# Five engines in hand-written order, load casts on GpSimd, unit 2 loaded ahead of the last weight piece, units 6 and 7 transposed by DMA: chunked attention followed by a bilinear FFN

## The chip, the cores and the metric

One core of one Trainium2 chip. The metric is the device time of one execution in microseconds (us). Traces and profiles are of one execution each. Their span is some 2 us shorter than the device time (338.6 against about 340.4 us for the kernel before).

## The reference

```python
# q, k, v: [8, 8, 576, 64] float32; w_a, w_b: [512, 1536]; w_out: [1536, 512]
q_c, k_c, v_c = (t.reshape(8, 8, 9, 64, 64) for t in (q, k, v))       # chunks of 64 tokens
scores = q_c @ k_c^T / 8
attn = softmax(scores)                                                # within a chunk
x = (attn @ v_c) put to [4608 tokens, 512]
return ((x @ w_a) * (x @ w_b)) @ w_out                                # float32
```

So there are 4608 tokens. The attention is small, and the three matrix products are nearly all of the arithmetic.

## The kernel before: the parts that matter here

Tokens go through in 18 *units* of 256 for the attention and in 9 *blocks* of 512 (two units each) for the FFN. For a unit, q, k and v are loaded in float32 and cast to bf16. Then q and k are transposed, either by TensorE through PSUM (units below `PE_UNITS`) or by the DMA queue. `scores`, `sums` and `values` are TensorE matmuls. Between them ScalarE takes exponents, the logarithm of the sums and the exponent of its negative, and VectorE multiplies. The result is the unit's half of `xT`. An `ab_step` makes one of twelve pieces of the hidden layer of a block: four matmuls each with w_b and w_a, an eviction on ScalarE and a product on VectorE. An `out_step` is twelve matmuls with w_out.

```python
    def cast_ab(i):                                   # a piece of the weights, 256 columns
        for n in ("wb", "wa"):
            w_ab[n, i] = wpool.tile([128, NKT, WCOL], BF16, name=f"{n}{i}")
            nc.vector.tensor_copy(out=w_ab[n, i], in_=staged.pop((n, i)))
    # ... (cast_wo likewise)
    def cast(U, names="qkv"):
        for n in names:
            raw[n, U] = raw_pool.tile([128, 2, H, D], BF16, name=f"{n}_raw", ...)
            eng = nc.vector if U < PE_UNITS else nc.gpsimd          # PE_UNITS = 8
            eng.tensor_copy(out=raw[n, U], in_=staged.pop((n, U)))

    def transpose_pe(U):
        # ... 8 transpositions of q, 8 of k into PSUM, then copies out:
            for i in range(2):
                cp = nc.vector.tensor_copy if w == 0 else nc.scalar.copy
                cp(out=dst[:, i], in_=tp[:, i].rearrange("c m (g p) -> c m g p", g=2))

    def slot(s=None, f=None):                         # scores of unit s, the rest of unit f
        # ... sums(f); scores(s); values(f)

    # Only TensorE and the sync queue follow the program; the other engines' order
    # is chosen by a scheduler when the program is built.
    with tc.manual_schedule(engines={mybir.EngineType.PE, mybir.EngineType.SP}):
        load_qk(0); load_qk(1); load_v(0); load_v(1)            # (one per line in the file)
        for i in range(3):
            load_ab(i)
        cast(0, "qk")
        transpose_pe(0)
        slot(0)
        cast(1, "qk")
        transpose_pe(1)
        cast(0, "v")
        slot(1, 0)
        cast(1, "v")
        cast_ab(0)
        slot(None, 1)
        for i in range(NWP):                                    # NWP = 6: block 0
            # ... cast_ab(i + 1), load_ab(i + 3), load(2) and load(3) at i == 3
            ab_step(0, 2 * i)
            if i == 5:
                # ... loads of w_out
                load(4)
                cast(2, "qk")
                load_qk(5)
                transpose_pe(2)
            ab_step(0, 2 * i + 1)
        slot(2)                                                 # unit 2, alone
        cast(2, "v")
        load_v(5)
        slot(None, 2)
        # ... block 1 in halves of 256 columns, with units 3 to 6 in between; blocks 2 to 8
```

The softmax here doesn't subtract the row's maximum and nothing guards it: scores larger than these inputs give would overflow.

## Time and profile before

| | before |
|---|---|
| device time, median (range) | 340.86 us (340.47 to 341.51, 3 runs) |
| span of the profiled execution | 338.6 us |
| TensorE busy | 313.0 us, 92% |
| VectorE, ScalarE, GpSimd busy | 158.9, 129.8, 31.9 us |
| first projection matmul | 22.31 us |
| one block of 512 tokens, blocks 3 to 7 | 33.2 us |

In the profile, PE is TensorE, DVE is VectorE, ACT is ScalarE, POOL is GpSimd and SPq is the sync queue, which issues the DMAs. L280 are the projection matmuls (`ab_step`), L296 the output matmuls, L164 the transpositions, L194, L209 and L232 the scores, sums and values.

The page of the kernel before starts with busy times per engine. Below them, one digit stands for the busy tenths of each of 40 equal slices of the span. PEclk is the granted TensorE clock in tenths.

```profile
PE 313.0 (92%) x2709; PEld 160.6 (47%) x2744; DVE 158.9 (47%) x251; ACT 129.8 (38%) x227; POOL 31.9 (9%) x36
...
PE   2459959999999999999999999999999999999994
...
PEclk9999996999999999999999999999999999999999
```

TensorE is nearly full from slice 7 on. The holes are in the first three slices (to 25 us) and in slice 6 (42 to 51 us), and in slice 7 the clock drops. The steady part has no hole. These lines are from the chain that ended last of the kernel before (start us, length us, what), from the sums of one unit to those of the next unit but one. The sums return every 33.17 us.

```profile
119.26 0.34 PE ps L209 x4
...
152.43 0.34 PE ps L209 x4
```

The start of the kernel before is in its timeline (start us, length us, engine, line, operation, output<-input, count; in brackets the idle time just before and what ended it).

```profile
7.74 0.69 DVE L152 CAST q_raw<-q_in 128x1024 bf16<-128x1024 f32 x1 [0.82 <-DMA q_in<-in_q_dram]
8.05 1.32 ACT L172 COPY qkt<-ps 128x512 bf16<-128x512 bf16 x2 [6.03 <-PE ps L164]
9.28 0.69 DVE L152 CAST k_raw<-k_in 128x1024 bf16<-128x1024 f32 x1 [0.84 <-DMA k_in<-in_k_dram]
...
9.88 1.32 DVE L172 COPY qkt<-ps 128x512 bf16<-128x512 bf16 x2
...
11.26 0.64 PE L194 MATMUL ps<-qkt 64*64 64x64 bf16 x32 [3.25 <-DVE qkt L172]
...
22.31 0.59 PE L280 MATMUL ps<-xT,wb_307 128*128 128x512 bf16 x1 [3.10 <-DVE xT L241]
```

The two casts at 7.74 and 9.28 are of unit 1. VectorE does them, and waits for the loads of them, while unit 0's transposed q lies ready in PSUM. Its copy runs only at 9.88, and TensorE's first scores wait for it.

Between blocks 0 and 1, the timeline of TensorE before shows unit 2 alone.

```profile
45.56 0.45 PE L194 MATMUL ps<-qkt 64*64 64x64 bf16 x32
...
46.70 0.90 PE L209 MATMUL ps<-E,ones 64*64 64x512 bf16 x4 [0.69 <-ACT E L202]
...
47.20 0.65 PE L232 MATMUL ps<-E,v_raw 64*64 64x64 bf16 x32
...
51.14 1.01 PE L280 MATMUL ps<-xT,wb_307 128*128 128x256 bf16 x4 [3.30 <-DVE xT L241]
```

The windows view of the kernel before (columns: stretch, its length, busy us and count per engine from PE to POOL, granted clock, DMA share, GB/s) gives the clock of that hole and of the stretch behind it.

```profile
47.80:51.10 3.30, 0.04 (x5) 0.07 (x1) 1.30 (x3) 1.94 (x3) 0.00 (x0) 0.74 1.06 406
51.10:56.40 5.30, 5.26 (x28) 3.79 (x28) 2.04 (x4) 1.12 (x3) 0.00 (x0) 0.52 1.21 257
```

So there are three things to see: two waits of TensorE (0.69 and 3.30 us), and after them 5.3 us in which it is busy but at half its clock.

### The profile page before, as it was taken

How to read it: one execution, taken by the hardware profiler on the slowest of the kernel's cores; microseconds unless marked ns; L12 is line 12 of the kernel's file. 1: busy time of each engine (PE TensorE's matmuls, PEld its weight loads, DVE VectorE, ACT ScalarE, POOL GpSimd, SP SyncE). 2: the span in 40 equal slices, each digit the busy share in tenths (PEclk: the TensorE clock that was granted, in tenths of full speed). 3: DMA queues.
4: the chain of work that ended last, by engine and by line, in shares of the span. 5: the costliest groups of instructions: out<-in, count | busy, mean ns of one | idle time of the engine just before them, and what ended most of it. 6: DMA issues, size and time to landing. Idle time of an engine off the chain costs nothing.

```text
span 338.6 us, 6687 instructions
## 1 busy us (share of the span) xinstructions
PE 313.0 (92%) x2709; PEld 160.6 (47%) x2744; DVE 158.9 (47%) x251; ACT 129.8 (38%) x227; POOL 31.9 (9%) x36
## 2 busy tenths in 40 slices
PE   2459959999999999999999999999999999999994
PEld 1324437876644444444444444444444444444441
DVE  2558665876854343435343434343435343533331
ACT  2643363645635162516341633253334424312200
POOL 0000000000333213312212130000000000000000
PEclk9999996999999999999999999999999999999999
DMA  8999999949999999998839863241111112011213
GB/s 238 328 345 286 255 375 230 290 107 260 222 238 220 192 217 244 232 219 187 199 70 202 204 157 75 52 95 33 31 37 27 33 31 48 16 31 45 50 32 93
DMA packets 130783, 52.87 MB, mean 156 GB/s; under 512 B 102080, under 2 KB 124608, under 8 KB 130752
## 3 DMA queue, kind: packets, MB, share of 16 engines
q1 hardware_dynamic: 130752, 52.44, 63.5%
q8 instruction: 21, 0.34, 0.4%
q14 instruction: 10, 0.08, 0.1%
HBM read 37.75 MB, written 9.44 MB: 139 GB/s over the span
## 4 chain that ended last, share of the span: by engine, by line
PE 90%; ACT 3%; DMA 2%; DVE 1%; issue 1%; SPq 1%
PE ps L280 56%; PE ps L296 27%; PE ps L164 2%; DMA k_in<-in_k_dram 2%; PE ps L209 2%; PE ps L194 2%; PE ps L232 1%; ACT rs L222 1%; ACT ln L219 1%; ACT qkt L172 1%; SPq L128 1%; DVE xT L241 1%; ACT E L202 0%; DVE qkt L172 0%; DVE k_raw L152 0%
## 5 line engine op out<-in xcount | busy, mean ns | idle before, releaser
L288 ACT CAST b_sb<-ps 128x512 bf16<-128x512 f32 (+1 forms) x120 | 64.3, 546 | 145.3 <-PE ps L280 121.6
L289 DVE TENSOR_TENSOR ab_sb<-ps,b_sb 128x512 bf16<-128x512 f32 (+1 forms) x120 | 75.6, 637 | 82.9 <-PE ps L280 80.2
L296 PEld LDWEIGHTS <-ab_sb 128*128 128x128 bf16 x432 | 42.2, 98 | 49.9
L304 DVE COPY o_sb<-ps 128x512 f32<-128x512 f32 x36 | 24.9, 691 | 54.8 <-PE ps L296 54.8
L241 DVE TENSOR_TENSOR xT<-ps,rs 128x512 bf16<-128x512 f32 x36 | 23.2, 686 | 30.1 <-ACT rs L222 30.1
L219 ACT ACTIVATE ln<-ps 128x512 f32<-128x512 f32 x36 | 19.7, 602 | 24.5 <-PE ps L209 24.5
L280 PE MATMUL ps<-xT,wb_307 128*128 128x512 bf16 (+1 forms) x79 | 20.3, 381 | 6.6 <-DVE xT L241 6.4
L152 POOL CAST q_raw<-q_in 128x1024 bf16<-128x1024 f32 x10 | 10.4, 1040 | 145.3 <-DMA q_in<-in_q_dram 130.2
L296 PE MATMUL ps<-wo_964,ab_sb 128*128 128x512 bf16 x72 | 21.4, 379 | 0.3
L296 PE MATMUL ps<-wo_1007,ab_sb 128*128 128x512 bf16 x72 | 21.4, 379 | 0.1
L296 PE MATMUL ps<-wo_1022,ab_sb 128*128 128x512 bf16 x72 | 21.4, 379 | 0.0
L296 PE MATMUL ps<-wo_992,ab_sb 128*128 128x512 bf16 x71 | 21.2, 379 | 0.0
L202 ACT ACTIVATE E<-ps 128x512 bf16<-128x512 f32 x36 | 19.3, 586 | 3.5 <-PE ps L194 3.5
L280 PE MATMUL ps<-xT,wa_309 128*128 128x512 bf16 (+1 forms) x80 | 20.5, 383 | 0.0
L296 PE MATMUL ps<-wo_949,ab_sb 128*128 128x512 bf16 x66 | 20.1, 379 | 0.3
L296 PE MATMUL ps<-wo_934,ab_sb 128*128 128x512 bf16 x67 | 20.3, 379 | 0.0
L280 PE MATMUL ps<-xT,wb_358 128*128 128x512 bf16 (+1 forms) x74 | 19.0, 365 | 0.3
L222 ACT ACTIVATE rs<-ln 128x1024 f32<-128x1024 f32 x18 | 19.0, 1057 | 0.6
L280 PE MATMUL ps<-xT,wa_360 128*128 128x512 bf16 (+1 forms) x80 | 19.2, 365 | 0.0
L280 PE MATMUL ps<-xT,wa_429 128*128 128x512 bf16 (+1 forms) x80 | 18.8, 358 | 0.4
L280 PE MATMUL ps<-xT,wb_461 128*128 128x512 bf16 (+1 forms) x74 | 18.6, 357 | 0.4
L280 PE MATMUL ps<-xT,wb_393 128*128 128x512 bf16 (+1 forms) x80 | 18.8, 358 | 0.0
(60 smaller groups left out, 325.7 us busy)
## 6 DMA issues: line engine op xcount, KB each, us to landing
out_dram<-o_sb SPq DMA_DIRECT2D x72, 128.0 KB, 2.4
v_in<-in_v_dram SPq DMA_DIRECT2D x32, 256.0 KB, 4.8
q_in<-in_q_dram SPq DMA_DIRECT2D x20, 256.0 KB, 4.4
k_in<-in_k_dram SPq DMA_DIRECT2D x20, 256.0 KB, 4.0
wst<-in_moe_w_b_dram SPq DMA_DIRECT2D x6, 512.0 KB, 9.4
wst<-in_moe_w_a_dram SPq DMA_DIRECT2D x6, 512.0 KB, 6.8
wst<-in_moe_w_out_dram SPq DMA_DIRECT2D x6, 512.0 KB, 8.3
q_in<-in_q_dram SPq DMA_DIRECT2D x5, 512.0 KB, 5.6
```

The costliest lines, as they stand in the source:

```text
L152: eng.tensor_copy(out=raw[n, U], in_=staged.pop((n, U)))
L164: nc.tensor.transpose(tp[:, i, m, :], src[:, i, 2 * m:2 * m + 2, :].rearrange("p j d -> p (j d)"), identity,)
L194: nc.tensor.matmul(sc[j][cl * 64:cl * 64 + 64, m, g, :], t[j * 64:j * 64 + 64, 1, g, m, cl * 64:cl * 64 + 64], t[j * 64:j * 64 + 64, 0, g, ...
L202: nc.scalar.activation(out=E_of[U][:, j], in_=sc[j], func=AF.Exp, scale=scale)
L219: nc.scalar.activation(out=ln[:, cl].rearrange("p m n -> p (m n)"), in_=sm[cl], func=AF.Ln)
L222: nc.scalar.activation(out=rs_of[U], in_=ln, func=AF.Exp, scale=-1.0)
L241: nc.vector.tensor_tensor(out=x_tiles[K][:, :, c0:c0 + 128], in0=av[cl].rearrange("p m g s -> p m (g s)"), in1=rs[:, cl], op=MULT,)
L280: nc.tensor.matmul(ps[n], w_ab[n, i][:, kt, o:o + 128], xT[:, kt, c0:c1], start=(kt == 0), stop=(kt == NKT - 1),)
L288: nc.scalar.copy(out=b_sb[:, :c1 - c0], in_=ps["wb"])
L289: nc.vector.tensor_tensor(out=ab_tiles[K][:, ft, c0:c1], in0=ps["wa"], in1=b_sb[:, :c1 - c0], op=MULT)
L296: nc.tensor.matmul(o_ps, ab_tiles[K][:, ft, tg * 128:tg * 128 + 128], w_out[ft], start=(ft == 0), stop=(ft == NFT - 1),)
L304: nc.vector.tensor_copy(out=o_sb, in_=o_ps)
```

## The change

Its intent is to remove TensorE's holes before 100 us. There are four parts:

- The program order is imposed on VectorE, ScalarE and GpSimd too.
- All casts of loads except unit 0's q and k go to GpSimd.
- Unit 2's q and k are loaded ahead of the last weight piece, so that unit 2 can be transposed, scored and valued inside block 0.
- Units 6 and 7 are transposed by the DMA queue.

Two smaller edits at the start go with them: VectorE copies unit 1's transposed k too, and the reciprocals of units 0 to 2 are made in two halves.

The diff, cut to its core:

```diff
-PE_UNITS = 8
+PE_UNITS = 6
...
-            nc.vector.tensor_copy(out=w_ab[n, i], in_=staged.pop((n, i)))
+            nc.gpsimd.tensor_copy(out=w_ab[n, i], in_=staged.pop((n, i)))
...  (cast_wo likewise)
-            eng = nc.vector if U < PE_UNITS else nc.gpsimd
+            eng = nc.vector if U == 0 and n != "v" else nc.gpsimd
...
-                cp = nc.vector.tensor_copy if w == 0 else nc.scalar.copy
+                cp = nc.vector.tensor_copy if w == 0 or U == 1 else nc.scalar.copy
...  (sums: for units 0 to 2 the reciprocal is made in two halves)
-    with tc.manual_schedule(engines={mybir.EngineType.PE, mybir.EngineType.SP}):
+    with tc.manual_schedule(
+        engines={
+            mybir.EngineType.PE, mybir.EngineType.SP, mybir.EngineType.DVE,
+            mybir.EngineType.Activation, mybir.EngineType.Pool,
+        }
+    ):
...
+        load(2, "qk")
+        load_ab(5)
+        load(2, "v")
+        load(3)
+        cast(2, "qk")
+        cast_ab(5)
+        cast(2, "v")
...
+        for ft in range(NFT):
+            ab_step(0, ft)
+            if ft == 7:
+                transpose_pe(2)
+            if ft == 8:
+                slot(2)
+            if ft == 10:
+                slot(None, 2)
...
+        for U in range(PE_UNITS, 8):
+            bring(U)                 # cast on GpSimd, transposition by DMA, next loads
...  (block 1: units 3 to 5 at new places, no cast in between)
```

More of the change, by code (lines that the diff above doesn't have):

```diff
@@ L95, in cast_wo @@
         t = wpool.tile([128, 2, DM], BF16, name=f"wo{i}")
-        nc.vector.tensor_copy(out=t, in_=staged.pop(("wo", i)))
+        nc.gpsimd.tensor_copy(out=t, in_=staged.pop(("wo", i)))
         for f in range(2):
@@ L120, in load_natural, with load @@
                 r, s, m = r + n, s + n, m - n
-    def load_qk(U):
-        for n, src in (("q", q), ("k", k)):
-            if U < PE_UNITS:
+    def load(U, names="qkv"):
+        for n in names if U < NU else "":
+            src = {"q": q, "k": k, "v": v}[n]
+            if U < PE_UNITS and n != "v":
                 st = in_pool.tile([128, H, 2, D], FP32, name=f"{n}_in")
@@ L135, in load_qk @@
                 load_natural(staged[n, U], src, U)
-    def load_v(U):
-        staged["v", U] = in_pool.tile([128, 2, H, D], FP32, name="v_in")
-        load_natural(staged["v", U], v, U)
-    def load(U):
-        if U < NU and ("q", U) not in staged:
-            load_qk(U)
-            load_v(U)
     def cast(U, names="qkv"):
-        for n in names:
+        for n in names if U < NU else "":
             raw[n, U] = raw_pool.tile(
@@ L221, in sums @@
             )
-        nc.scalar.activation(out=rs_of[U], in_=ln, func=AF.Exp, scale=-1.0)
+            if U < 3:
+                nc.scalar.activation(out=rs_of[U][:, cl], in_=ln[:, cl], func=AF.Exp, scale=-1.0)
+        if U >= 3:
+            nc.scalar.activation(out=rs_of[U], in_=ln, func=AF.Exp, scale=-1.0)
     def values(U):
@@ L226, in values @@
         K, u = divmod(U, 2)
+        if u == 0:
+            x_tiles[K] = x_pool.tile([128, NKT, BLK], BF16, name="xT")
         av = [bank().rearrange("p (m g s) -> p m g s", m=NKT, g=2) for _ in range(2)]
@@ L251, in slot @@
             s = None
-        if s is not None and s % 2 == 0:
-            x_tiles[s // 2] = x_pool.tile([128, NKT, BLK], BF16, name="xT")
         if f is not None:
@@ L261, in bring @@
     def bring(U):
+        cast(U, "qk")
+        load(U + 1, "q")
         if U < NU:
-            cast(U)
             transpose_dma(U)
-        load(U + 2)
+        cast(U, "v")
+        load(U + 1, "kv")
     ab_tiles = {}
@@ L309, in out_step @@
             nc.sync.dma_start(out=out[r0:r0 + 64, :], in_=o_sb[g * 64:g * 64 + 64, :])
-    with tc.manual_schedule(engines={mybir.EngineType.PE, mybir.EngineType.SP}):
-        load_qk(0)
-        load_qk(1)
-        load_v(0)
-        load_v(1)
+    with tc.manual_schedule(
+        engines={
+            mybir.EngineType.PE,
+            mybir.EngineType.SP,
+            mybir.EngineType.DVE,
+            mybir.EngineType.Activation,
+            mybir.EngineType.Pool,
+        }
+    ):
+        load(0, "qk")
+        load(1, "qk")
+        load(0, "v")
+        load(1, "v")
         for i in range(3):
@@ L320 @@
         transpose_pe(0)
-        slot(0)
         cast(1, "qk")
-        transpose_pe(1)
-        cast(0, "v")
-        slot(1, 0)
-        cast(1, "v")
-        cast_ab(0)
-        slot(None, 1)
-        for i in range(NWP):
-            if i + 1 < NWP:
-                cast_ab(i + 1)
-            if i + 3 < NWP:
-                load_ab(i + 3)
-            if i == 3:
-                load(2)
-                load(3)
-            ab_step(0, 2 * i)
-            if i == 5:
-                for j in range(6):
-                    load_wo(j)
-                load(4)
-                cast(2, "qk")
-                load_qk(5)
-                transpose_pe(2)
-            ab_step(0, 2 * i + 1)
-        slot(2)
-        cast(2, "v")
-        load_v(5)
-        slot(None, 2)
-        def qk(U):
-            cast(U, "qk")
-            load_qk(U + 3)
-            transpose_pe(U)
-        def vs(U):
-            cast(U, "v")
-            load_v(U + 3)
+        cast(0, "v")
+        cast(1, "v")
+        for i in range(NWP - 1):
+            cast_ab(i)
+            if i < 2:
+                load_ab(i + 3)
+        scores(0)
+        transpose_pe(1)
+        sums(0)
+        scores(1)
+        values(0)
+        sums(1)
+        values(1)
+        load(2, "qk")
[5 more added lines that the diff above has]
+        cast(2, "v")
+        cast(3)
+        for j in range(6):
+            load_wo(j)
+        for j in range(6):
+            cast_wo(j)
+        load(4)
+        load(5)
+        for ft in range(NFT):
+            ab_step(0, ft)
+            if ft == 7:
+                transpose_pe(2)
+            if ft == 8:
+                slot(2)
+            if ft == 10:
+                slot(None, 2)
+        cast(4)
+        cast(5)
+        load(6)
+        for U in range(PE_UNITS, 8):
+            bring(U)
         seq = [lambda ft=ft: ab_step(1, ft, 0, 256) for ft in range(NFT)]
@@ L363 @@
         for at, f in reversed([
-            (3, lambda: qk(3)),
-            (5, lambda: slot(3)),
-            (7, lambda: vs(3)),
-            (8, lambda: slot(None, 3)),
-            (8, lambda: cast_wo(0)),
-            (9, lambda: cast_wo(1)),
-            (10, lambda: cast_wo(2)),
-            (12, lambda: cast_wo(3)),
-            (13, lambda: cast_wo(4)),
-            (14, lambda: cast_wo(5)),
+            (1, lambda: transpose_pe(3)),
+            (4, lambda: slot(3)),
+            (7, lambda: slot(None, 3)),
             (16, lambda: out_step(0, 0)),
-            (16, lambda: qk(4)),
+            (16, lambda: transpose_pe(4)),
             (18, lambda: slot(4)),
-            (18, lambda: vs(4)),
             (20, lambda: out_step(0, 1)),
-            (20, lambda: qk(5)),
+            (20, lambda: transpose_pe(5)),
             (21, lambda: slot(5, 4)),
-            (21, lambda: vs(5)),
             (22, lambda: out_step(0, 2)),
-            (22, lambda: qk(6)),
             (23, lambda: slot(6, 5)),
-            (23, lambda: vs(6)),
             (24, lambda: out_step(0, 3)),
@@ L398 @@
                 seq.insert(4, lambda: slot(2 * K + 3, 2 * K + 2))
+                seq.insert(0, lambda: bring(2 * K + 5))
                 if K == 2:
-                    seq.insert(2, lambda: bring(9))
-                    seq.insert(2, lambda: bring(8))
-                    seq.insert(2, lambda: (qk(7), vs(7)))
-                else:
-                    seq.insert(0, lambda: bring(2 * K + 5))
+                    seq.insert(0, lambda: bring(8))
             for step in seq:
```

## The prediction

> **What bounds it.** TensorE: the table of engines gives PE 313.0 of 338.6 us. The chain of waits shows a steady 33.2 us per 512-token block (120.20, 153.37, 186.54, ...), matmuls 0.216 us apart, no hole. The listing of waits gives PE only some 19 us, all early. The other engines have room.
>
> What is lost lies before 100 us (timeline):
> 1. Start: the first projection matmul runs at 22.31 us. VectorE casts q and k of unit 1 (7.74, 9.28) before it copies unit 0's transposed q (9.88 to 11.2); that copy alone holds the first scores (11.26).
> 2. Between blocks 0 and 1, unit 2 runs with nothing beside it: PE idle 0.7 us, then 47.85 to 51.14 (3.3 us, waiting for xT).
> 3. After that hole the first 24 matmuls of 256 columns take 5.2 us; later ones 0.109 us each (2.6 us for 24). The windows view shows a granted clock of 0.50 there. The Trainium skill (TensorE: Matmul & The Clock Gate, Part 1) says an idle window of about 3.4 us halves the clock; this trace agrees.
> 4. Units 6 and 7 transpose on PE, 0.9 us each, and wait some 0.2 us each for copies.
>
> **What the change does.**
> - Start: VectorE copies unit 0's q at once; GpSimd casts q/k of unit 1 (1.04 us against 0.69) and all later loads. Estimate from these durations: scores of unit 0 at 9.4, of unit 1 at 13.5, last xT 19.2, first projection 19.4. Saves 2.9.
> - Unit 2's q and k come ahead of the last weight piece: transposed after step 7, scored after 8, valued after 10. Its xT takes about 3.4 us after its sums (two ln of 0.60, two half exps of about 0.55, products of 0.69), covered by values and one step of 1.73. Hole about 0.9 instead of 4.0: saves 3.1.
> - That hole is too short to halve the clock: saves 2.6.
> - Units 6, 7 by DMA (3 us each, off PE): saves 1.8, and 0.4 of waits on copies.
> - Added: 70 GpSimd casts of 1.04 us, about 20 us of work in the first 40.
> - Weights: pieces 0 to 2 land at about 17 to 23 us; the queue was saturated (share about 1.0, about 300 GB/s) and carries the same bytes. Unit 2's q/k should be cast by 33 us, needed at 35.
> - Fixed order on ScalarE and VectorE in blocks 2 to 8: no change, PE is full.
>
> Sum: 2.9 + 3.1 + 2.6 + 1.8 + 0.4 = 10.8 us, all on the critical path. 340.9 - 10.8 = **330.0 us**, range 327.0 to 334.0. Faster by over 2%: 0.90; within 2%: 0.09; slower: 0.01.
>
> **What would show it.** First projection matmul at 19 to 20 us; block 1's first matmul near 45 instead of 51, with a gap of about 1 us and matmuls at 0.109 us at once (granted clock near 1.00); 12 instead of 10 q and k DMA transposes; blocks still 33.2 us; GpSimd casts near 1.04 us.
>
> **What would make it wrong.** GpSimd's order: a cast that waits for its load holds up the weights behind it, so PE waits in block 0. The sync queue waiting for a cast of unit 7 holds up loads and stores. A hole that still halves the clock (+2.6). In-order ScalarE delaying evictions so that PE lacks PSUM banks in every block.

## The result

| | before | after |
|---|---|---|
| device time, median (range) | 340.75 us (340.47 to 341.51, 4 runs) | 330.86 us (330.27 to 331.51, 4 runs) |
| ratio, 95% interval | | 0.9707 (0.9683 to 0.9731) |
| span | 338.6 | 329.1 us |
| VectorE, ScalarE, GpSimd busy | 158.9, 129.8, 31.9 | 133.9, 126.7, 73.7 us |

A ratio is the mean time of one kernel's runs over the mean of the other's runs of the same rounds, so it is not quite the ratio of the medians quoted. The kernel after was run a second time later, on chip 4, with the ratio 0.9696. The experiments ran on chips 3, 1, 4 and 0, each beside the kernel before on the same chip, so they are compared by their ratios to it. Where a difference from the kernel after is given below in us, it is the difference of the ratios (against 0.9702, the middle of those two) times 340.9 us. An interval of a ratio is about 0.002 to 0.003 each way, which is 0.7 to 1.0 us.

In the kernel after, L278 are the projection matmuls, L294 the output matmuls, L156 the transpositions, and L186, L201 and L230 scores, sums and values. The same lines of the page after:

```profile
PE 311.4 (95%) x2712; PEld 157.4 (48%) x2712; DVE 133.9 (41%) x209; ACT 126.7 (38%) x224; POOL 73.7 (22%) x76
...
PE   2669989999999999999999999999999999999994
...
PEclk9999999999999999999999999999999999999999
```

The thin place of slice 6 is nearly gone (8 instead of 5 tenths), and so is the dip of the clock. The start in the timeline after:

```profile
6.74 1.32 DVE L164 COPY qkt<-ps 128x512 bf16<-128x512 bf16 x2
...
7.70 1.04 POOL L144 CAST q_raw<-q_in 128x1024 bf16<-128x1024 f32 x1 [6.39 <-DMA q_in<-in_q_dram]
...
9.32 0.64 PE L186 MATMUL ps<-qkt 64*64 64x64 bf16 x32 [1.41 <-ACT qkt L164]
...
19.65 1.87 PE L278 MATMUL ps<-xT,wb_162 128*128 128x512 bf16 x4 [2.74 <-DVE xT L239]
```

VectorE now copies unit 0's q at 6.74, GpSimd casts unit 1's, and the first scores wait for ScalarE's copy of k alone. The seam of blocks 0 and 1 in the timeline of TensorE after:

```profile
42.34 0.41 PE L201 MATMUL ps<-E,ones 64*64 64x512 bf16 x4
42.58 0.48 PE L230 MATMUL ps<-E,v_raw 64*64 64x64 bf16 x32
42.98 1.04 PE L278 MATMUL ps<-xT,wb_409 128*128 128x512 bf16 x4
43.86 1.03 PE L278 MATMUL ps<-xT,wa_411 128*128 128x512 bf16 x4
45.99 0.60 PE L278 MATMUL ps<-xT,wb_162 128*128 128x256 bf16 x4 [1.11 <-DVE xT L239]
46.43 0.60 PE L278 MATMUL ps<-xT,wa_164 128*128 128x256 bf16 x4
```

The wait for xT is 1.11 us, and the next group of four starts 0.44 us later, which is 0.109 us per matmul. The windows view after shows the clock there:

```profile
44.00:46.00 2.00, 0.89 (x6) 0.30 (x4) 1.45 (x3) 1.66 (x4) 1.40 (x2) 1.00 1.05 402
46.00:50.00 4.00, 4.00 (x45) 3.68 (x45) 2.70 (x6) 2.21 (x5) 2.23 (x3) 1.00 1.06 405
```

And the chain after in the steady part: the sums return every 33.17 us, as before.

```profile
125.37 0.34 PE ps L201 x4
...
158.55 0.34 PE ps L201 x4
```

Where the time came from, by the starts of the same piece of work in the two traces (us):

| start of | before | after | gained so far |
|---|---|---|---|
| first projection matmul | 22.31 | 19.65 | 2.66 |
| 13th projection matmul | 26.44 | 24.47 | 1.97 |
| block 1 | 51.14 | 45.99 | 5.15 |
| first output step of block 0 | 69.69 | 62.09 | 7.60 |
| block 2 | 93.15 | 84.33 | 8.82 |
| sums of unit 6, in block 2 | 101.81 | 92.10 | 9.71 |
| end of the span | 338.6 | 329.1 | 9.5 |

All of the gain is there by 92 us. The second row is a step back: the first twelve matmuls took 4.13 us before and 4.82 us after, against 2.6 us at 0.216 us each. They run at half speed at first in both kernels, and the slow stretch was longer in this trace of the kernel after.

### The profile page after: what moved, and what is told of

Read it like the earlier page. It is cut to its first block, busy times and chain, and to the rows that moved or that the text cites. A ratio compares the mean times of both kernels' runs of the same rounds, so it can differ in the third digit from the quotient of the medians.

```text
span 329.1 us, 6671 instructions
## 1 busy us (share of the span) xinstructions
PE 311.4 (95%) x2712; PEld 157.4 (48%) x2712; DVE 133.9 (41%) x209; ACT 126.7 (38%) x224; POOL 73.7 (22%) x76
## 4 chain that ended last, share of the span: by engine, by line
PE 93%; ACT 3%; DMA 1%; DVE 1%; issue 0%; SPq 0%
PE ps L278 57%; PE ps L294 28%; PE ps L201 2%; PE ps L156 2%; PE ps L186 2%; PE ps L230 1%; DMA k_in<-in_k_dram 1%; ACT rs L216 1%; ACT ln L212 1%; ACT qkt L164 1%; DVE xT L239 0%; DVE k_raw L144 0%; DVE o_sb L302 0%; ACT E L194 0%; SPq L129 0%
## 5 line engine op out<-in xcount | busy, mean ns | idle before, releaser
L294 PEld LDWEIGHTS <-ab_sb 128*128 128x128 bf16 x432 | 42.3, 98 | 50.1
L239 DVE TENSOR_TENSOR xT<-ps,rs 128x512 bf16<-128x512 f32 x36 | 23.4, 687 | 32.3 <-ACT rs L218 27.6
L144 POOL CAST q_raw<-q_in 128x1024 bf16<-128x1024 f32 x17 | 17.7, 1042 | 60.3 <-DMA q_in<-in_q_dram 52.0
L144 POOL CAST k_raw<-k_in 128x1024 bf16<-128x1024 f32 x17 | 17.7, 1042 | 47.9 <-DMA k_in<-in_k_dram 47.7
L278 PE MATMUL ps<-xT,wb_162 128*128 128x512 bf16 (+1 forms) x80 | 20.2, 378 | 3.8 <-DVE xT L239 3.8
L144 POOL CAST v_raw<-v_in 128x1024 bf16<-128x1024 f32 x18 | 18.8, 1042 | 17.7 <-DMA v_in<-in_v_dram 13.3
L294 PE MATMUL ps<-wo_437,ab_sb 128*128 128x512 bf16 x72 | 21.4, 379 | 0.0
L294 PE MATMUL ps<-wo_443,ab_sb 128*128 128x512 bf16 x72 | 21.4, 379 | 0.0
L294 PE MATMUL ps<-wo_433,ab_sb 128*128 128x512 bf16 x72 | 21.4, 379 | 0.0
L294 PE MATMUL ps<-wo_439,ab_sb 128*128 128x512 bf16 x72 | 21.4, 379 | 0.0
L294 PE MATMUL ps<-wo_441,ab_sb 128*128 128x512 bf16 x72 | 21.4, 379 | 0.0
L294 PE MATMUL ps<-wo_435,ab_sb 128*128 128x512 bf16 x72 | 21.4, 379 | 0.0
L278 PE MATMUL ps<-xT,wa_164 128*128 128x512 bf16 (+1 forms) x80 | 19.7, 370 | 0.0
L278 PE MATMUL ps<-xT,wb_186 128*128 128x512 bf16 (+1 forms) x80 | 18.9, 359 | 0.0
L278 PE MATMUL ps<-xT,wb_170 128*128 128x512 bf16 (+1 forms) x80 | 18.9, 359 | 0.0
L278 PE MATMUL ps<-xT,wb_182 128*128 128x512 bf16 (+1 forms) x80 | 18.8, 358 | 0.0
L278 PE MATMUL ps<-xT,wb_409 128*128 128x512 bf16 (+1 forms) x80 | 18.8, 358 | 0.0
```

Of the source, the lines that this page charges most:

```text
L239: nc.vector.tensor_tensor(out=x_tiles[K][:, :, c0:c0 + 128], in0=av[cl].rearrange("p m g s -> p m (g s)"), in1=rs[:, cl], op=MULT,)
L278: nc.tensor.matmul(ps[n], w_ab[n, i][:, kt, o:o + 128], xT[:, kt, c0:c1], start=(kt == 0), stop=(kt == NKT - 1),)
L294: nc.tensor.matmul(o_ps, ab_tiles[K][:, ft, tg * 128:tg * 128 + 128], w_out[ft], start=(ft == 0), stop=(ft == NFT - 1),)
```

## The experiments

Theory A is that of the prediction: the gain is a sum of separate shifts of TensorE's stream. The shifts are the start (VectorE's order), the hole at unit 2, the half clock behind that hole, and the transpositions of units 6 and 7. Rival B says that the hand-fixed order of the engines is the gain. Rival C says that taking some 25 us of casts off VectorE is the gain.

### e1_pe8: units 6 and 7 back on TensorE

```diff
-PE_UNITS = 6
+PE_UNITS = 8
-        for U in range(PE_UNITS, 8):
-            bring(U)
+        for U in (6, 7):
+            cast(U)
+            load(U + 1)
+            (22, lambda: transpose_pe(6)),          # in block 1
+                    seq.insert(2, lambda: transpose_pe(7))   # in block 2
```

> The change as given, but units 6 and 7 are transposed on TensorE again (their loads in the layout for it, one transposition after the third output step of block 0, one in block 2). Theory A (the gain is a sum of separate shifts of TensorE's stream: start, hole at unit 2, clock after it, transpositions): 1.8 us of TensorE time plus up to 0.4 us of waits come back, so 332.6 to 333.1 us against 330.9. Rival B (the fixed order of the engines and the move of casts to GpSimd make the gain; where 6 and 7 are transposed is nothing, as TensorE had slack): 330.9 within 0.3.

Measured: 332.99 us, ratio 0.9768 (0.9745 to 0.9791), so +2.3 us on the kernel after. Both transpositions stand in the chain that ended last of e1_pe8 (start us, length us, what):

```profile
79.89 0.91 PE ps L156 x16
...
89.97 0.89 PE ps L156 x16
```

From the start of block 1 to the sums of unit 6 in block 2 its trace takes 48.23 us (46.95 to 95.18), against 46.11 in the kernel after. That is 2.12 us more: 1.80 us of transpositions and 0.3 us beside them. So theory A's sum for this part holds. These transpositions were on the critical path, because TensorE had no slack at either place.

### e2_hole and e3_hole_filled: the hole at unit 2, and its clock

```diff
 # e2_hole
-            if ft == 7:
-                transpose_pe(2)
-            if ft == 8:
-                slot(2)
-            if ft == 10:
-                slot(None, 2)
+            if ft == 10:
+                transpose_pe(2)
+        slot(2)
+        slot(None, 2)
 # e3_hole_filled: the same, and then
+        filler(13, 512)     # 13 matmuls of 512 columns into a PSUM bank that nobody reads
```

> The change as given, but unit 2 is transposed after step 10 and scored, summed and valued after step 11 of block 0, as in the kernel before. Theory A: the hole of about 4 us between blocks 0 and 1 and the half clock behind it return: hole from 1.1 to about 4 us (+2.9) and 24 matmuls of 256 columns at about 0.21 us (+2.4), so 336.0 to 336.6 us, granted clock near 0.5 just after the hole. Rival B: within 1 us of 330.9, since casts and orders are as in the change.

> As e2_hole, but 13 matmuls of 512 columns whose result nobody reads (about 2.8 us) fill TensorE's wait for xT behind the hole's attention. They add no wait to anything else. If the idle time in the hole is what halves the clock, as theory A has it, block 1 starts at once at 0.109 us per 256 columns and the time is about 2.4 us below e2_hole, 333.5 to 334.2 us. If the slow matmuls behind the hole have another cause (late weights, xT, banks), the time equals e2_hole within 0.5 us.

Measured: e2_hole 335.68 us, ratio 0.9841 (0.9818 to 0.9864), so +4.7 us. e3_hole_filled 333.65 us, ratio 0.9781 (0.976 to 0.9802), so +2.7 us. The timelines of TensorE, first e2_hole:

```profile
47.98 1.01 PE L278 MATMUL ps<-xT,wb 128*128 128x256 bf16 x4 [2.93 <-DVE xT L239]
48.78 1.06 PE L278 MATMUL ps<-xT,wa 128*128 128x256 bf16 x4
49.63 1.06 PE L156 MATMUL ps<-identity,q_raw 128*128 128x128 bf16 x8
```

then e3_hole_filled, whose L315 are the fillers:

```profile
45.11 2.98 PE L315 MATMUL ps<-wb,identity 128*128 128x512 bf16 x13
48.11 0.60 PE L278 MATMUL ps<-xT,wb 128*128 128x256 bf16 x4
48.54 0.60 PE L278 MATMUL ps<-xT,wa 128*128 128x256 bf16 x4
```

Block 1 starts within 0.13 us of the same time in both. Behind the idle hole four matmuls take 0.80 to 0.85 us; behind the filled hole they take 0.43 us. Late weights or a late xT cannot be the cause: both blocks start at the same time, and behind the idle hole the transpositions of unit 3 are as slow as the projections. So it is TensorE's idleness that halves the clock. The fillers, which compute nothing, win back 2.0 us of the time. e2_hole came out a little under what was expected (+5.1 to +5.7). In the one profiled run of e2_hole the slow stretch at the start of block 0 was 0.8 us shorter than after, which hides part of the loss in that run. Whether it explains the median is not shown.

### e4_auto: ScalarE and VectorE ordered by the scheduler

```diff
-            mybir.EngineType.DVE,
-            mybir.EngineType.Activation,
```

> The change as given, but the order of ScalarE and VectorE is left to the scheduler (only TensorE, GpSimd and the sync queue are fixed). Theory A: in blocks 2 to 8 the order of these two doesn't matter, and at the start the casts that held up VectorE are on GpSimd anyway, so 330.4 to 332.0 us. Rival B (the hand-fixed order of these engines is the gain): several us of it go, 334 us or more.

Measured: 332.27 us, ratio 0.9738 (0.971 to 0.9765), so +1.2 us. The intervals of the two kernels overlap, but the trace shows a place. Its span is 1.6 us longer, all of it in block 1: at the start of block 1 it was even (45.84 against 45.99 us), and the period of the steady part is the same 33.17 us. In the timeline of e4_auto VectorE takes the copies of unit 3's transposed q three products later:

```profile
50.83 1.32 DVE L164 COPY qkt<-ps 128x512 bf16<-128x512 bf16 x2
...
52.21 0.45 PE L186 MATMUL ps<-qkt 64*64 64x64 bf16 x32 [1.83 <-DVE qkt L164]
```

In the kernel after, that copy runs at 47.51 us and the scores at 50.47 us without a wait. So the fixed order does matter at this place in the trace. In the time it is worth about 1 us, which the overlapping intervals do not settle. Rival B as the whole explanation falls, as far as ScalarE and VectorE go: it wanted 334 us or more. GpSimd's order stayed fixed in this run, and no run frees it alone.

### e5_before_u1 and e9_before_pool: casts moved in the kernel before

```diff
 # e5_before_u1: the kernel before, with only
-            eng = nc.vector if U < PE_UNITS else nc.gpsimd
+            eng = nc.vector if U < PE_UNITS and (U != 1 or n == "v") else nc.gpsimd
 # e9_before_pool: the kernel before, with only
+            eng = nc.vector if U == 0 and n != "v" else nc.gpsimd
+            nc.gpsimd.tensor_copy(...)      # in cast_ab and cast_wo too
```

> The kernel before with one part of the change alone: unit 1's q and k are cast on GpSimd instead of VectorE; nothing else. Theory A (at the start, VectorE's casts of unit 1 stand in front of the copy of unit 0's transposed q, and that copy holds the first scores): unit 0's scores move from 11.26 to about 9.4 us and the first projection matmul from 22.31 to about 20.0 to 20.5 us, so 1.8 to 2.3 us less, about 338.5 to 339.0. If the start is held by something else (landing of q and k, or of the weights): no more than 0.5 us.

> The kernel before with all casts of loads but unit 0's q and k on GpSimd, as the change has them, and nothing else of the change (order of program, fixed engines, place of unit 2 and transpositions as before). Theory A: only the start's gain, 1.5 to 3 us, so 337.8 to 339.4 us, with the hole of about 4 us and the half clock behind it still there. Rival C (taking some 25 us of casts off VectorE is most of the gain): 334 us or less.

Measured: e5_before_u1 339.57 us, ratio 0.9956 (0.9937 to 0.9975), 1.5 us less than before. e9_before_pool 338.78 us, ratio 0.9935 (0.992 to 0.995), 2.2 us less. The timeline of e5_before_u1 shows the mechanism:

```profile
6.79 1.33 DVE L172 COPY qkt<-ps 128x512 bf16<-128x512 bf16 x2
...
9.38 0.64 PE L194 MATMUL ps<-qkt 64*64 64x64 bf16 x32 [1.41 <-ACT qkt L172]
...
20.43 1.87 PE L280 MATMUL ps<-xT,wb 128*128 128x512 bf16 x4 [3.10 <-DVE xT L241]
```

Two casts on another engine move the first scores from 11.26 to 9.38 us, and the first projection by 1.88 us. Part of that is eaten by a longer slow stretch right behind it (4.63 us for the first twelve projection matmuls instead of 4.13), so that the time falls by 1.5 us. In the kernel after, the first projection comes another 0.78 us earlier (19.65). That goes with the rest of the change at the start, such as the reciprocals in halves, and no run tests it alone. Moving all the other casts as well adds about 0.7 us, within the noise, so rival C falls too. VectorE had idle time, and only the order at the start mattered. In both runs the hole before block 1 is still there (3.3 us).

### e6_warm: TensorE kept busy before the first projection

```diff
+        filler(36)              # matmuls of 128 columns that nobody reads
         cast(0, "qk")
         transpose_pe(0)
+        filler(8)
...
         sums(0)
+        filler(8)
         scores(1)
         values(0)
+        filler(5)
         sums(1)
         values(1)
+        filler(32)
```

> The change as given, plus matmuls of 128 columns whose result nobody reads on TensorE in the waits before the first projection: 36 before the first transposition, 8, 8 and 5 in the waits of the attention of units 0 and 1, 32 behind it. Theory A on the clock: TensorE then comes warm to the first projection, its first 12 matmuls take 2.6 instead of 4.8 us, and the attention's own matmuls shorten, so 2 to 4 us less, 327 to 329 us. If the slow matmuls at the start are not the clock's idle state: no gain, or a loss of up to 2 us where a filler runs past the wait.

Measured: 331.98 us, ratio 0.9739 (0.9718 to 0.9759), so +1.3 us: the expected gain did not come. The first part did come. The first projection is at 18.41 us, its matmuls run at full speed at once, and the 13th matmul is at 20.99 us instead of 24.47, so TensorE is 3.5 us ahead. The listing of waits of e6_warm (who waited for whom, total us, times, longest) shows where it went:

```profile
PE ps L156 <- POOL q_raw L144: 2.3, 1, 2.3
...
PE ps L156 <- POOL k_raw L144: 1.8, 2, 1.3
```

TensorE reaches unit 2's transpositions at about 32.3 us, and the cast of its q and k ends only at 34.6 and 36.6 us. The two waits for them take 2.26 and 1.35 us, more than the lead (the other wait in the second line is one of unit 1). Afterwards TensorE was slow again (first matmuls behind that wait 0.43 us apart). The loads themselves came later than in the kernel after: by the trace, the last piece of unit 2's k landed at 35.4 us instead of 33.0. The delay is older than these loads. The first piece of w_a was cast at 17.99 us instead of 16.77, and the sync queue issued unit 2's q at 24.16 instead of 21.45.

### e7_vals9 and e8_vals9_swap: the rest of the hole, and the waits for copies

```diff
 # both
-            if ft == 10:
+            if ft == 9:
                 slot(None, 2)
 # e8_vals9_swap also
-            (16, lambda: out_step(0, 0)),
             (16, lambda: transpose_pe(4)),
+            (16, lambda: out_step(0, 0)),
...  (the same for transpose_pe(5) and out_step(0, 1))
```

> The change as given, but unit 2's sums and values come after step 9 of block 0 instead of step 10. Theory A: the hole left between blocks 0 and 1 (1.1 us) is only the time from unit 2's sums to its xT, which now has two steps (3.5 us) to hide behind, so it closes: 1.0 to 1.1 us less, 329.8 us. If v of unit 2 or its scores come too late for that, TensorE waits at the sums instead and the gain is smaller or none.

> The change with unit 2's sums and values after step 9 (as in e7_vals9), and with the transpositions of units 4 and 5 before the output steps of block 0 beside them instead of after. Theory A: the copies of unit 5's transposed k then hide behind 2.6 us of output matmuls, so about 0.3 us of waits at 73 to 74.6 us go as well, 328.9 us; if unit 5's loads come too late for the earlier place, TensorE waits there and the gain is lost.

Measured: e7_vals9 329.19 us, ratio 0.9656 (0.9636 to 0.9676), so -1.6 us. e8_vals9_swap 329.71 us, ratio 0.9663 (0.9643 to 0.9684), so 1.1 us less than the kernel after run beside it (0.9696). In e7_vals9 the wait before block 1 is gone:

```profile
44.05 1.03 PE L278 MATMUL ps<-xT,wa 128*128 128x512 bf16 x4
44.91 0.60 PE L278 MATMUL ps<-xT,wb 128*128 128x256 bf16 x4
```

That confirms that the 1.11 us was only the time from unit 2's sums to its xT. The gain is 0.5 us above what was expected, which is within the noise. In e8_vals9_swap the waits for transposed copies in block 1 vanish from the listing, but its time is no better than e7_vals9's. A gain of 0.3 us is below what these rounds resolve, so this is inconclusive.

### e11_after_again: the kernel after, beside the next ones

No edit.

> The kernel after the change, unaltered, run again beside the next two on the same chip: 330.9 us within 0.7.

Measured: 330.82 us (330.05 to 331.40), ratio 0.9696 (0.9677 to 0.9715). In its trace the first twelve projection matmuls took 5.07 us (19.82 to 24.89), against 4.82 us in the other trace of the same kernel, and between 3.92 (e3_hole_filled) and 5.07 us in the other kernels whose start has no filler. The length of the slow stretch differs from run to run. The upper figure is a cap: where the twelve took 5.07 us (here, in e1_pe8 and in e4_auto), the next few matmuls were slow too.

### e10_fill_last and e12_fill_first: a smaller filler

```diff
 # e10_fill_last: e8_vals9_swap, and
         values(1)
+        filler(24)
 # e12_fill_first: e10_fill_last, and
+        filler(36)
         cast(0, "qk")
```

> As e8_vals9_swap, with 24 matmuls of 128 columns whose result nobody reads in the wait of 2.7 us just before the first projection (2.6 us even at half clock, so they delay nothing). If the half clock at the first projection comes from that wait and the loose work before it, up to 2 us are gained by the first 12 matmuls. But e6_warm showed that unit 2's q and k land just in time for the slower TensorE: most of it should come back as a wait for those casts in front of unit 2's transpositions, so in all 0 to 1 us less than e8_vals9_swap, 328.0 to 328.9 us, not 2 us.

> As e10_fill_last (ratio to before 0.962, last piece of unit 2's k landed at 33.2 us), plus 36 matmuls of 128 columns that nobody reads from 1.4 to 5.4 us, before the first transposition. In e6_warm the same 36 and 21 more in the attention's waits were there, and the loads were late: unit 2's k landed at 35.4 us and TensorE waited 3.6 us for it. If the 36 early matmuls make the loads late, k of unit 2 lands near 35 us again, TensorE waits for it, and the time is 2 us or more above e10_fill_last (ratio 0.968 or more). If not, the attention of units 0 and 1 starts warm, k lands near 33 us and the ratio is 0.958 to 0.963.

Measured: e10_fill_last 328.11 us (327.49 to 328.89), ratio 0.9623 (0.9602 to 0.9643). That is 2.5 us less than the kernel after on the same chip and about 1.4 us less than e8_vals9_swap, so more came through than the 0 to 1 us that I had expected, though the difference is within the noise. Its timeline:

```profile
16.90 2.74 PE L313 MATMUL ps<-identity 128*128 128x128 bf16 x24
19.70 1.23 PE L278 MATMUL ps<-xT,wb 128*128 128x512 bf16 x3
20.77 1.03 PE L278 MATMUL ps<-xT,wa 128*128 128x512 bf16 x4
```

The fillers end as xT arrives. The slow stretch shrinks to the first few matmuls, and the 13th starts at 22.5 instead of 24.5 us. My expectation that most of this returns as a wait for unit 2's q and k was wrong at this size. TensorE came to unit 2's transpositions at 33.7 us, when q was there, and k held it up by only 0.3 us. e10_fill_last has the lowest ratio, and so is the fastest version and gives correct results.

e12_fill_first: 328.98 us, but from 327.52 to 331.66, ratio 0.9642 (0.9612 to 0.9672). The 36 early matmuls do not make the loads late: in its trace the first of the two loads of unit 2's k landed at 32.0 us, against 33.9 us in e6_warm, and TensorE waited 1.1 us for the cast. The ratio lies between the two expected ranges, but the loads decide. Nor did the attention stay at full speed: the granted clock on record is 0.50 from 8.6 to 12.0 and from 15.4 to 18.8 us. So the late loads of e6_warm have another cause, which I did not find. Nor is it a gain. The spread is large, and its profiled run, the slowest of six, also waited 1.8 us for the DMA transposition of a unit's k.

## Why the prediction was right

The predicted 330.0 us lies within 0.9 us of the measured 330.86 us, and its steps can be checked one by one. The mechanism was right: separate shifts of TensorE's stream, all before 100 us, that add up.

- **Start, 2.9 us.** The first projection moved by 2.66 us. Unit 0's scores came at 9.32 us (predicted 9.4) and unit 1's at 13.59 us (13.5). e5_before_u1 shows the cause of the scores' shift by itself: two casts moved, first scores at 9.38 us. It accounts for 1.88 of the 2.66 us; the other 0.78 us was not tested alone.
- **Hole at unit 2, 3.1 us.** The waits fell from 0.69 and 3.30 us to 1.11 us, a gain of 2.9 us. e2_hole brings the hole back, and e7_vals9 closes the rest of it by giving xT one step more to hide behind.
- **Half clock behind it, 2.6 us.** Gone in the trace after. e3_hole_filled is the proof that idle time and not late data was its cause, with a gain of 2.0 us in time and slow matmuls behind the idle hole alone. The reason given for the hole that is left, that it is too short, came out right, but the length of a single wait is not the whole rule (see the last section).
- **Transpositions of units 6 and 7, 1.8 and 0.4 us.** e1_pe8 costs 2.3 us.
- **No change in the steady part.** 33.17 us per block in both chains.
- **GpSimd's load.** 70 casts, 1.042 us each, as predicted. Unit 2's k was cast by 34.1 us (predicted 33), and needed at about 36 us. The DMA queue made 12 transpositions each of q and k instead of 10, as predicted.

Two terms were missing or mis-sized. The prediction has no term for the slow stretch at the first projection, and so takes it to be as long after as before. In the two traces the first twelve matmuls took 4.82 us instead of 4.13, which gave back 0.7 us of the start's 2.66 and would be most of the 0.9 us between prediction and result. And "fixed order on ScalarE and VectorE: no change" was said of blocks 2 to 8, where it held. Block 1 was not considered, and e4_auto shows about 1.2 us there, too near the noise to be sure of in the time, but visible as a wait of 1.83 us in the trace. If both are real, one loss and one gain were left out that partly cancel, so some of the closeness of the predicted number is luck.

The parts measured in separate runs make up the whole within the noise: e9_before_pool 2.2, e2_hole 4.7 (of which 2.0 the clock) and e1_pe8 2.3 us give 9.2 us, and e4_auto's order 1.2 us. The change as a whole gives 10.0 to 10.4 us (ratios 0.9707 and 0.9696).

What stays open is why the loads of e6_warm landed late (unit 2's k by 2.4 us, and weights before it). It is also open what sets the length of the slow stretch at the start; the traces here show 3.9 to 5.1 us for the first twelve matmuls where no filler runs before them, in both the kernel before (4.13) and the variants of the kernel after.

## What to carry to other kernels

When the main engine is 92% busy, do not look at its average. Find the few places where it waits, and cost each by the wait and by the slow clock behind it; a wait of 3 us cost another 2 us here, and useless matmuls in the wait won those back. A helper engine with time to spare can still hold up everything by the order of its work: two early casts in front of one copy cost 1.9 us at the start, while moving the other casts, 23 us of the same engine's busy time, gained only 0.7 us, within the noise. When a hole has been closed, check what else had been just in time: making TensorE 3.5 us earlier ran it into loads that had not been waited for until then.

## What the Trainium skill lacked or had wrong

- "TensorE: Matmul & The Clock Gate", Part 1, puts the return to half clock after an idle window of about 3.4 us. The trace agrees only roughly: 3.30 us of idle time were followed by half speed, and the single wait of 1.11 us was not. The prediction's "this trace agrees" holds in that sense only. But the window need not be idle all through. In the kernel before, the granted clock on record fell at 49.4 us, only 1.5 us after unit 2's last matmul, and TensorE had been busy for 1.06 of the 3.41 us before. In e2_hole it fell at 46.4 us, with 1.20 us of work in the 3.41 us before, and also at 15.7 us, with 1.12 us of work and no wait longer than 1.23 us. At the seam of the kernel after, the 3.4 us up to the end of its wait held 2.29 us of work, and the clock stayed. So the advice in the page's last section, no gaps above about 3 us, is too generous here: two waits of some 1.1 us close together were enough. How much work keeps the clock up is not shown.
- The same page warns that its clock events can be unreliable in traces. The runs add a case: from 20 to 25 us the windows view of the kernel after gives a granted clock of 1.00, while the matmuls of 512 columns start 0.43 us apart until about 23.9 us. Only e2_hole's record shows a fall before its first projection among the runs without fillers at the start. There the clock reads 0.50 from 15.8 to 22.5 us, and the projection matmuls are slow until then. The spacing of the matmuls is the safer reading.
- The same page, Part 4, gives 275 to 390 ns for a transposition of 128x128 on TensorE, and says that the full clock does not engage for it. Here 16 of them (`nc.tensor.transpose` in the kernel; the trace does not tell the mode) take 0.89 us in a stream, 0.056 us from one to the next, at full clock, and 0.107 us behind the idle hole of e2_hole. So the clock does act on these. The spacing in a stream is not the length of one alone, so it does not contradict the page's 275 to 390 ns.
- "GPSIMD Engine Reference", section 4.1, calls work with one input roughly line-rate on GpSimd. It has no figure for a cast from float32 to bf16: 128x1024 elements took 1.042 us on GpSimd and 0.686 us on VectorE.
- "TensorE: Matmul & The Clock Gate" advises warming up with matmuls for benchmarks (its last section), and restructuring the loop for kernels that wait (Part 1). It does not name the remedy tried here inside a kernel, filling a known wait with unread matmuls: 13 of 512 columns won 2.0 us (e3_hole_filled), 24 of 128 columns about 1.4 us, about the size of the noise of two ratios (e10_fill_last), and 89 of them spread over the start none (e6_warm).
